# Batch 0's front of a sketched-attention kernel, rearranged: kv before the denominators, nine outer-product columns on GpSimd, one w_out product left whole

## The chip, the cores and the metric

The kernel runs on one core of a Trainium2 chip. The metric is the device time of one execution, in microseconds (us); several executions are timed and their median is given. A core has five engines with queues of their own: TensorE (PE; its weight loads are listed as PEld), VectorE (DVE), ScalarE (ACT), GpSimd (POOL) and SyncE (SP, which here only issues DMAs). Each takes its instructions in the order of the program and waits on semaphores for the other engines' results and for DMA landings.

## The reference

Polynomial-sketch attention, then a gated feed-forward layer with a sigmoid gate:

```python
# q, k, v: (4 batches, 4 heads, 1088 tokens, 32); S1, S2: (8, 32)
def phi(x):                       # 64 features a token
    a = einsum('rd,bhsd->bhsr', S1, x)
    b = einsum('rd,bhsd->bhsr', S2, x)
    return einsum('bhsi,bhsj->bhsij', a, b).reshape(..., 64)
q_p, k_p = phi(q), phi(k)
kv  = einsum('bhsf,bhsd->bhfd', k_p, v)
z   = sum(k_p, axis=2)
num = einsum('bhsf,bhfd->bhsd', q_p, kv)
den = einsum('bhsf,bhf->bhs', q_p, z)[..., None] + 1e-06
x   = (num / den) as (4352 tokens, 128)
gate = 1 / (1 + exp(-(x @ w_gate)));  val = x @ w_val    # w: (128, 1536)
out = (gate * val) @ w_out                               # w_out: (1536, 128)
```

The inputs arrive as 64-bit floats. The kernel loads them as pairs of 32-bit words; for S1, S2 and the three weight matrices it builds 32-bit floats from both words.

## The kernel before

**Staging.** The attention of a batch gives 1088 columns of `xT` (128 channels by 4352 tokens). The feed-forward layer walks over the tokens in chunks of 512 and, within a chunk, over 12 blocks of 128 hidden units. One step of it is a wave (`w1`, L556): gate and val products of a block for a chunk, then the sigmoid on ACT (`sg`, L564), the product `g` on DVE (L599), and later the block's w_out product. For the first chunk that is `w2` (L425), into the PSUM tile `moeout`; for the others it is a scheme with fewer products (L381). `slot` deals out waves one by one between pieces of the next batches' attention. A w_out product of the first chunk is emitted two waves after its own wave.

**Order.** The order within PE, DVE, ACT and POOL is that of the program text. The DMAs of SP stand in the order of their emission too. The start, batch 0, is written out by hand and is what the change rearranges.

**Loads.** The loads of the start go out on SP (k on ACT's queue): S, q's first 16 rows a partition (`T0`), gate and val of block 0, v in four parts, gate and val of block 1, w_out of blocks 0 and 1 (`load_w_out(0)`), q's other 18 rows, and then, for each pair of blocks, gate, val and w_out.

**Batch 0's front**, in the order of the text:
- `turn_q(0, 0)` turns q's first half on DVE (L673); `kps` multiplies k by the sketches (L693) and turns the results on DVE (L703) into `kab`, one half for each pair of heads.
- `ab` makes the sketches of q in PSUM (`aps`, `bps`, L800); ACT copies the first (`asb`, L810), DVE multiplies the two (`mult00`, `mult10`, L819) into `qp`.
- `gram` (L716) makes, with `spread_z` and `mask_z`, batch 0's z: ACT's copy `gs`, POOL's masking `gh` (L727), a spreading matmul (L739), then DVE's `zm` and `zb` (L750, L762).
- `outer` (L772) makes the 64 features of k for columns j0 to j1 of the nine that one pair of heads has (`kp`, 128 elements a column): by default on DVE, or on POOL.
- `kv0` (L899) adds up v times `kp` into `kvz`, for each column one matmul for each of the four heads; `kvd` copies the result (ACT, L934), `ndt` turns it on PE (`ndps`, L968) and copies it (`nd`, L985).
- `dn(0, 0, rest)` makes the denominators of the first 512 tokens (`dps`, L1083), calls `rest`, and makes the numerators (`nps`, L1102). `rest` holds the turn of the denominators (`dT`, L1094), their copy with eps (`rc`, L1224) and steps of the weights' conversion. `divide` then takes the reciprocal (L1116), spreads it (`rb`, L1131) and writes two halves of `xT` (L1121), with `head1` between.
- `head1` holds the turn of q's second half, conversion steps, and `qcomp` and `spread`: a product of q's second half with the sketches (`cqps`, L839), its copy (`cq`, L847), and four DMAs by way of DRAM (one out, three back) that make the operands of `qmult(0, 1)` (L892), which comes much later.

**Conversion of the weights.** `step(name, n)` runs one step on part n. Parts 0 and 1 are gate and val of blocks 0 and 1, part 2 is w_out of both, part 3 and every further one are the three matrices of one block (part 3 is block 2). The steps: `bounds` (ACT L140, then POOL L141), `lower` (ACT L152; for part 3 DVE L148), `shift` (DVE L157), `total` (POOL L162), `sign` (ACT L168), `final` (DVE L171, writes `w_sb`). A wave waits for its block's `final`.

Of the kernel before, what the change touches and what calls it, by code (L numbers as in the profile page):

```python
# [16 lines left out]
P = 128  # L17
# [3 lines left out]
def kernel(  # L21
# [12 lines left out]
    nc = tc.nc  # L34

    B, H, S, D = q.shape
# [4 lines left out]
    NJ = DFF // P  # L41
# [4 lines left out]
    NJK = 9  # L46
# [146 lines left out]
    def load_w_in(j0, j1):  # L193
        cs = slice(j0 * P, j1 * P)
        n, jj = divmod(j0, 2)
        if wide and jj == 0:
            w_in[n] = raw.tile([P, 3, 2, P, 2], I32, tag="w_in", name="w_in")
        for i, src in enumerate((moe_w_gate, moe_w_val)):
            if wide:
                nc.sync.dma_start(  # L200
                    out=w_in[n][:, i, jj : jj + j1 - j0].rearrange("p j m w -> p (j m w)"),
                    in_=src[:, cs].bitcast(I32),
                )
            else:
                nc.sync.dma_start(
                    out=w_sb[:, i, j0:j1].rearrange("p j m -> p (j m)"), in_=src[:, cs]
                )

    def load_w_out(n):
        j0, j1 = 2 * n, 2 * n + 2  # L210
        cs = slice(j0 * P, j1 * P)
        src = moe_w_out[cs, :].bitcast(I32) if wide else moe_w_out[cs, :]
        nc.sync.dma_start(
            out=w_in[n][:, 2].rearrange("p j m w -> p j (m w)") if wide else w_sb[:, 2, j0:j1],
            in_=src.rearrange("(j p) m -> p j m", p=P),
        )
# [26 lines left out]
    def load_rows(src, b, t, parts=((0, T, nc.sync),)):  # L243
        for t0, t1, eng in parts:
            eng.dma_start(
                out=t[:, t0:t1, :],
                in_=bass.AP(
                    tensor=src.tensor,
                    offset=src[b, 0].offset + t0 * D,
                    ap=[[T * D, P], [1, (t1 - t0) * D]],  # L250
                ),
            )
# [33 lines left out]
    load_w_in(0, 1)  # L286
    load_v(0)
    load_w_in(1, 2)
    load_w_out(0)
    load_rows(q, 0, q_t[0], ((T0, T, nc.sync),))  # L290
    for n in range(1, NJ // 2):
        load_w_in(2 * n, 2 * n + 2)
        load_w_out(n)
# [124 lines left out]
    def w2(ci, j0, jn, g):  # L418
        if j0 == 0:
            moe["sum"] = ci  # L420
            moe["acc"] = pso.tile([P, TCH], F32, tag="acc0", name="moeout")
        for jj in range(jn):
            j = j0 + jj
            for d in (slice(0, P),) if j < NJ - 2 else (slice(0, 64), slice(64, P)):
                nc.tensor.matmul(  # L425
                    out=moe["acc"][d],
                    lhsT=w_sb[:, 2, j, d],
                    rhs=g[:, jj],
                    start=(j == 0),
                    stop=(j == NJ - 1),  # L430
                )
        if j0 + jn == NJ:
            o_sb = sbA.tile([P, TCH // 32, 32], F32, tag="o_sb", name="o_sb")
            nc.vector.transpose(out=o_sb.rearrange("p t d -> p (t d)"), in_=moe["acc"])
            moe["store"] = lambda: store(
                ci, lambda g4: o_sb[32 * g4 : 32 * g4 + 32], nc.scalar
            )
# [245 lines left out]
    def kps(b):  # L683
        t = ps2.tile([P, 2, 512], F32, tag="two", name="kps")
        ts = [t[:, 0], t[:, 1]]
        turns = [(g, pi) for g in range(4) for pi in range(2)]

        if b == 0:
            ts[1] = pso.tile([P, TCH], F32, tag="acc1", name="kps1")
            turns.sort(key=lambda x: x[1])  # L690
        for g, pi in turns:
            rows = slice(64 * pi, 64 * pi + 64)
            nc.tensor.matmul(  # L693
                out=ts[pi][32 * g : 32 * g + 32, : NJK * 32],
                lhsT=sk[rows, :],
                rhs=kT_of[b][rows, KBASE[g] : KBASE[g] + NJK],
                start=True,
                stop=True,
            )

        KAB[b] = sbA.tile([P, 2, NJK, 32], F32, tag="kab", name="kab")
        for pi in range(2):
            nc.vector.transpose(  # L703
                out=KAB[b][:, pi].rearrange("p j c -> p (j c)"), in_=ts[pi][:, : NJK * 32]
            )
        KP[b] = sbA.tile([P, 2, NJK, 2, F], F32, tag="kp", name="kp", bufs=1)
# [62 lines left out]
    def outer(b, pi, j0=0, j1=NJK, eng=nc.vector):  # L769
        a0 = KAB[b][:, pi, j0:j1]  # L770
        ap = [list(a0.ap[0]), [2 * R, 2 * (j1 - j0)]]
        eng.tensor_tensor(  # L772
            out=KP[b][:, pi, j0:j1].rearrange("p j m (i l) -> p (j m) i l", i=R),
            in0=bass.AP(tensor=a0.tensor, offset=a0.offset, ap=ap + [[1, R], [0, R]]),
            in1=bass.AP(tensor=a0.tensor, offset=a0.offset + R, ap=ap + [[0, R], [1, R]]),
            op=MUL,
        )
# [6 lines left out]
    def ab(a_of=None, b_of=None, pool_b=None):  # L784

        mm = []
        if a_of is not None:
            aps = psm.tile([P, 2, 512], F32, tag="wave", name="aps")
            mm.append((a_of, aps, sa))
        if b_of is not None:  # L790
            pool, tag = (ps2, "two") if pool_b is None else pool_b
            bps = pool.tile([P, 2, 512], F32, tag=tag, name="bps")
            mm.append((b_of, bps, sb))
        for c in range(2):
            for m in range(2):
                for (bb, pr, n), dst, sx in mm:
                    h = 2 * pr + m
                    rows = slice(32 * h, 32 * h + 32)
                    t0, tn = q_chk[n]
                    nc.tensor.matmul(  # L800
                        out=dst[64 * c : 64 * c + 64, m, : 32 * tn],
                        lhsT=sx[rows, :],
                        rhs=qT_of[bb][rows, t0 : t0 + tn, c, :],
                        start=True,
                        stop=True,
                    )
        if a_of is not None:
            w = 32 * q_chk[a_of[2]][1]
            ASB[a_of] = sbA.tile([P, 2, 256], F32, tag="asb", name="asb", bufs=2)
            nc.scalar.copy(out=ASB[a_of][:, :, :w], in_=aps[:, :, :w])  # L810
        if b_of is not None:

            def mult():
                bb, pr, n = b_of
                if bb not in QP:
                    QP[bb] = sbA.tile([P, 2 * H * W1], F32, tag="qp", name="qp")
                t0, tn = q_chk[n]
                w = 32 * tn
                nc.vector.tensor_tensor(  # L819
                    out=half(QP[bb], n).rearrange("p (m c) w -> p c m w", m=2)[:, pr],  # L820
                    in0=bps[:, :, :w],
                    in1=ASB[b_of][:, :, :w],
                    op=MUL,
                )

            return mult
# [64 lines left out]
        q0 = half(QP[b], n)  # L891
        nc.vector.tensor_tensor(out=q0, in0=q0, in1=half(BQ[b], n), op=MUL)  # L892

    def kv0(j_list):
        if 0 not in KVZ:
            KVZ[0] = pso.tile([P, TCH], F32, tag="acc1", name="kvz")
        for j in j_list:
            for h in range(H):
                nc.tensor.matmul(  # L899
                    out=KVZ[0][32 * h : 32 * h + 32, :F],  # L900
                    lhsT=v_sb[:, h, j, :],
                    rhs=KP[0][:, h // 2, j, h % 2, :],
                    start=(j == 1),
                    stop=(j == NJK - 1),
                    skip_group_check=True,
                )
# [290 lines left out]
    sa, sb = sab  # L1197
    turn_q(0, 0)
    kps(0)
    ab((0, 0, 0))  # L1200
    ab((0, 1, 0))
    spread_z, mask_z = gram()
    mult00 = ab(None, (0, 0, 0))
    mult10 = ab(None, (0, 1, 0), (psm, "wave"))
    for pi in range(2):
        outer(0, pi, NJK - 3, NJK, eng=nc.gpsimd)
    step("bounds", 0, 1)
    step("lower", 0, 1)
    spread_z()
    for pi in range(2):  # L1210
        outer(0, pi, 0, 5)
    kv0([1, 2, 3, 4, 0])
    mult00()
    mult10()
    mask_z()


    def rest(turn, rc, dT):
        for pi in range(2):
            outer(0, pi, 5, NJK - 3)  # L1220
        kv0(range(5, NJK))
        turn()
        nt = rc.shape[1] - 1
        nc.scalar.activation(out=rc[:, :nt], in_=dT[:, :nt, :2], func=ACTF.Identity, bias=eps)  # L1224
        kvd(0)
        step("shift", 0, 1)
        step("total", 0, 1)
        step("sign", 0, bank="acc0")
        ndt(0)

    divide = dn(0, 0, rest)

    def head1():
        turn_q(0, 1)
        step("final", 0)
        step("sign", 1, bank="acc1")
        step("bounds", 2)
        step("lower", 2)
        step("bounds", 3)
        spread(0, (1,), qcomp(0, (1,), (psm, "wave")), nc.sync, nc.sync)  # L1240

    divide((0, 4), (4, 8), between=head1)
    step("final", 1)
# [170 lines left out]
```

## Time and profile before

| | us |
|---|---|
| three runs, median (lowest to highest) | 290.52 (290.42 to 290.61) |
| the profiled execution's own time | 289.88 |
| its span, first to last instruction | 288.1 |
| PE busy in it, 2262 matmul records | 282.3 (98%) |
| DVE / ACT / POOL busy | 171.2 / 106.7 / 159.7 |

The granted TensorE clock was 1.00 throughout. A product in 32-bit floats shows as two matmul records, so that 512 columns take two records that start 0.43 us apart. Rows of the timeline begin with the start and the duration in us; "x2" merges neighbours of one kind, and a bracket at the end gives the engine's idle time before the row and what ended it.

Marks of the front: kps at 5.96, `kab`'s two turns at 6.72, DVE's outer products at 7.49, POOL's at 9.07, `zb` at 10.45, dps at 10.81, dT at 11.51, the first `xT` at 13.96, the first wave at 14.44, the first w_out product at 17.99, block 2's wave at 18.85.

### The profile page before, as it was taken

To read this page: it belongs to the slowest core of one execution; us is meant where nothing else is said; L and a number is where in the kernel's file an instruction comes from. 1 tells how busy PE (TensorE), PEld (TensorE's weight loads), DVE (VectorE), ACT (ScalarE), POOL (GpSimd) and SP (SyncE) were. 2 spreads that over 40 slices of the span, in tenths; PEclk is the share of its full clock that TensorE was granted. 3 is DMA by queue.
4 is the path that set the end of the run, shared out by engine and by line. 5 is a ranking of instruction groups with operands and counts; after the bars stand their busy time and mean duration, and the time that the engine had idled before them with its cause. 6 is when DMAs were issued, how large, how long until landed. Compare 5 with 4: busy or idle time off the path is not lost.

```text
span 288.1 us, 5789 instructions
## 1 busy us (share of the span) xinstructions
PE 282.3 (98%) x2262; PEld 134.4 (47%) x2262; DVE 171.2 (59%) x294; ACT 106.7 (37%) x215; POOL 159.7 (55%) x222
## 2 busy tenths in 40 slices
PE   8799999999999999999999999999999999999995
PEld 3454433354444444535444445444444444444685
DVE  6987788946748547668446485767245223522571
ACT  3788832222334322523244222532243224421341
POOL 2666682667466387383565496483564646555200
PEclk9999999999999999999999999999999999999999
DMA  7995441765700386451000673020001000020012
GB/s 215 338 371 122 111 156 43 167 143 126 207 2 2 77 192 155 108 164 29 1 0 12 159 181 102 2 30 9 0 3 23 14 2 0 4 35 1 0 19 40
DMA packets 28891, 24.24 MB, mean 84 GB/s; under 512 B 18560, under 2 KB 24064, under 8 KB 28864
## 3 DMA queue, kind: packets, MB, share of 16 engines
q1 hardware_dynamic: 25888, 22.10, 29.8%
q10 hardware_dynamic: 2976, 1.77, 2.1%
q8 instruction: 18, 0.29, 0.5%
q14 instruction: 9, 0.07, 0.1%
HBM read 20.60 MB, written 3.26 MB: 83 GB/s over the span
## 4 chain that ended last, share of the span: by engine, by line
PE 97%; ACT 1%; DVE 1%; issue 0%; POOL 0%
PE wave L556 61%; PE prod L381 22%; PE moeout L425 4%; PE moeout L451 2%; PE warm L301 2%; PE kvz L912 1%; PE nps L1271 1%; PE kps L693 1%; PE cqps L839 1%; PE nps L1102 0%; PE denj L1041 0%; PE dps L1083 0%; PE nps L1054 0%; ACT asb L810 0%; DVE qp L819 0%; PE aps L800 0%
## 5 line engine op out<-in xcount | busy, mean ns | idle before, releaser
L556 PE MATMUL wave<-xT,w_sb 128*64 128x512 f32 (+3 forms) x820 | 201.4, 565 | 0.0
L564 ACT ACTIVATE sg<-wave 128x512 f32<-128x512 f32 x102 | 60.9, 597 | 158.0 <-PE wave L556 152.0
L599 DVE TENSOR_TENSOR g<-wave,sg 128x512 f32<-128x512 f32 x96 | 66.0, 688 | 87.6 <-ACT sg L564 86.1
L371 POOL TENSOR_TENSOR tsum<-g,tsum 128x256 f32<-128x256 f32 x84 | 67.5, 804 | 71.0 <-DVE g L599 70.8
L556 PEld LDWEIGHTS wave<-xT,w_sb 128*64 128x64 f32 (+1 forms) x820 | 71.0, 140 | 72.5 <-issue 53.0
L371 POOL TENSOR_TENSOR tsum<-g 128x256 f32<-128x256 f32 x84 | 67.5, 804 | 22.3 <-DVE g L599 21.7
L381 PE MATMUL prod<-tsum,ws 128*64 128x256 f32 x252 | 68.4, 380 | 0.0
L381 PE MATMUL prod<-g,w_sb 128*64 128x256 f32 (+1 forms) x170 | 50.3, 378 | 0.0
L381 PEld LDWEIGHTS prod<-tsum,ws 128*64 128x64 f32 x252 | 34.0, 137 | 13.1 <-issue 9.7
L381 PEld LDWEIGHTS prod<-g,w_sb 128*64 128x64 f32 x170 | 23.0, 137 | 30.1 <-issue 25.8
L381 PE MATMUL prod<-tsum,w_sb 128*64 128x256 f32 x84 | 25.0, 380 | 0.0
L381 PE MATMUL prod<-g,ws 128*64 128x256 f32 x84 | 25.0, 379 | 0.0
L162 POOL TENSOR_TENSOR head<-head,tail 128x384 int32<-128x384 int32 (+1 forms) x13 | 13.2, 1022 | 4.3 <-DVE head L157 4.3
L381 PEld LDWEIGHTS prod<-g,ws 128*64 128x64 f32 x84 | 11.5, 137 | 5.7
L425 PE MATMUL moeout<-g,w_sb 128*128 128x512 f32 (+1 forms) x28 | 12.4, 600 | 0.0
L381 PEld LDWEIGHTS prod<-tsum,w_sb 128*64 128x64 f32 x84 | 11.3, 137 | 1.3 <-issue 1.0
L892 DVE TENSOR_TENSOR qp<-qp,bq 128x1152 f32<-128x1152 f32 (+1 forms) x7 | 10.5, 1502 | 0.3 <-DMA bq<-dq 0.3
L772 DVE TENSOR_TENSOR kp<-kab 128x1152 f32<-128x1152 f32 (+2 forms) x10 | 10.7, 1081 | 0.0
L592 DVE TENSOR_TENSOR g<-wave,sg 128x512 f32<-128x512 f32 x6 | 6.8, 1132 | 6.3 <-ACT sg L564 4.7
L496 DVE TENSOR_TENSOR res<-prod,other 128x256 f32<-128x256 f32 x14 | 5.9, 425 | 6.3 <-ACT other L487 4.8
L141 POOL TENSOR_SCALAR head<-cap 128x384 f32<-128x384 f32 (+1 forms) x13 | 6.3, 487 | 5.2 <-ACT cap L140 5.2
L152 ACT ACTIVATE tail<-w_in,two__157 128x384 f32<-128x384 uint32 (+1 forms) x12 | 7.2, 610 | 0.0
(130 smaller groups left out, 196.0 us busy)
## 6 DMA issues: line engine op xcount, KB each, us to landing
qp<-dq SPq DMA_DIRECT2D x7, 576.0 KB
bq<-dq SPq DMA_DIRECT2D x14, 288.0 KB
kq<-in_k_dram SPq DMA_DIRECT2D x3, 544.0 KB
kq<-in_q_dram SPq DMA_DIRECT2D x3, 544.0 KB
w_in<-in_moe_w_out_dram SPq DMA_DIRECT2D x6, 256.0 KB
w_in<-in_moe_w_gate_dram SPq DMA_DIRECT2D x5, 256.0 KB
w_in<-in_moe_w_val_dram SPq DMA_DIRECT2D x5, 256.0 KB
v<-in_v_dram SPq DMA_DIRECT2D x8, 144.0 KB
```

The costliest lines, as they stand in the source:

```text
L141: nc.gpsimd.tensor_scalar(out=self.head.bitcast(F32), in0=self.cap, scalar1=122880.0, scalar2=2.0**-15, op0=ALU.min, op1=ALU.max,)
L152: nc.scalar.activation(out=self.tail, in_=self.lo, func=ACTF.Identity, bias=two, scale=2.0**-51)
L162: nc.gpsimd.tensor_tensor(out=self.head, in0=self.head, in1=self.tail.bitcast(I32), op=ALU.add)
L371: nc.gpsimd.tensor_tensor(out=t[:, u], in0=in0, in1=in1, op=ALU.subtract)
L381: nc.tensor.matmul(out=out, lhsT=lhsT, rhs=rhs, start=start, stop=stop, skip_group_check=True)
L425: nc.tensor.matmul(out=moe["acc"][d], lhsT=w_sb[:, 2, j, d], rhs=g[:, jj], start=(j == 0), stop=(j == NJ - 1),)
L556: nc.tensor.matmul(out=wv[d, which, jj * tw + o : jj * tw + o + tp], lhsT=w_sb[:, which, j0 + jj, d], rhs=xT[:, t0 + o : t0 + o + tp], sta ...
L564: nc.scalar.activation(out=sg, in_=wv[:, 0], func=ACTF.Sigmoid)
L592: nc.vector.tensor_tensor(out=g.rearrange("p (j u s y) -> p j y u s", j=2, u=2, y=4), in0=wv[:, 1].rearrange("p (j y u s) -> p j y u s", j ...
L599: nc.vector.tensor_tensor(out=g, in0=wv[:, 1], in1=sg, op=MUL)
L772: eng.tensor_tensor(out=KP[b][:, pi, j0:j1].rearrange("p j m (i l) -> p (j m) i l", i=R), in0=bass.AP(tensor=a0.tensor, offset=a0.offset, ...
L892: nc.vector.tensor_tensor(out=q0, in0=q0, in1=half(BQ[b], n), op=MUL)
```

## The change

In words: q's second half is loaded before w_out of blocks 0 and 1. POOL makes columns 4 to 8 for the first pair of heads, ahead of `gh`, and columns 5 to 8 for the second pair after it; DVE makes the other nine in two instructions where it made twelve in four. All of `kv0` is emitted ahead of `dn`: columns 1, 2, 3 and 0 for all heads, then columns 4 to 8 for heads 0 and 1, then for heads 2 and 3. The turn of q's second half and `kvd` follow `mask_z`; `ndt` comes first in `rest`. In `head1`, `qcomp` and `spread` stand before `lower` of part 2 and `bounds` of part 3. In `w2`, only block 11's product is still made in two halves of 64 rows; block 10's is whole.

```diff
@@ loads
     load_w_in(1, 2)
+    load_rows(q, 0, q_t[0], ((T0, T, nc.sync),))
     load_w_out(0)
-    load_rows(q, 0, q_t[0], ((T0, T, nc.sync),))
@@ w2
-            for d in (slice(0, P),) if j < NJ - 2 else (slice(0, 64), slice(64, P)):
+            for d in (slice(0, P),) if j < NJ - 1 else (slice(0, 64), slice(64, P)):
@@ kv0
-    def kv0(j_list):
+    def kv0(j_list, heads=range(H)):
...
-            for h in range(H):
+            for h in heads:
@@ batch 0's front
     turn_q(0, 0)
     kps(0)
+
+    by_pool = (NJK - 5, NJK - 4)
+    outer(0, 0, by_pool[0], NJK, eng=nc.gpsimd)
     ab((0, 0, 0))
     ab((0, 1, 0))
     spread_z, mask_z = gram()
     mult00 = ab(None, (0, 0, 0))
     mult10 = ab(None, (0, 1, 0), (psm, "wave"))
-    for pi in range(2):
-        outer(0, pi, NJK - 3, NJK, eng=nc.gpsimd)
+    outer(0, 1, by_pool[1], NJK, eng=nc.gpsimd)
     step("bounds", 0, 1)
     step("lower", 0, 1)
     spread_z()
     for pi in range(2):
-        outer(0, pi, 0, 5)
-    kv0([1, 2, 3, 4, 0])
+        outer(0, pi, 0, by_pool[pi])
+    kv0([1, 2, 3, 0])
+    kv0(range(4, NJK), (0, 1))
+    kv0(range(4, NJK), (2, 3))
     mult00()
     mult10()
     mask_z()
+    turn_q(0, 1)
+    kvd(0)
 
     def rest(turn, rc, dT):
-        for pi in range(2):
-            outer(0, pi, 5, NJK - 3)
-        kv0(range(5, NJK))
+        ndt(0)
         turn()
...
-        kvd(0)
         step("shift", 0, 1)
         step("total", 0, 1)
         step("sign", 0, bank="acc0")
-        ndt(0)
...
     def head1():
-        turn_q(0, 1)
         step("final", 0)
         step("sign", 1, bank="acc1")
         step("bounds", 2)
+        spread(0, (1,), qcomp(0, (1,), (psm, "wave")), nc.sync, nc.sync)
         step("lower", 2)
         step("bounds", 3)
-        spread(0, (1,), qcomp(0, (1,), (psm, "wave")), nc.sync, nc.sync)
```

## The prediction

> **What bounds the kernel now.** First the chain that ended last: TensorE (PE) holds it for 97%, and its feed-forward lines L556, L381 and L425 alone make 87%. Then busy time by stretch, cut where the first feed-forward matmul starts (14.44 us), where block 2's wave starts (18.85) and where block 10's w_out product comes up (45.21). The columns are stretch, length, then busy us and count by engine, granted TensorE clock, DMA share and GB/s.
>
> ```profile
> 0.00:14.44 14.44, 11.94 (x201) 5.98 (x201) 11.71 (x37) 7.36 (x20) 6.31 (x21) 1.00 0.92 277
> 14.44:18.85 4.41, 4.41 (x19) 2.65 (x16) 3.88 (x10) 3.88 (x8) 2.75 (x5) 1.00 1.07 374
> 18.85:45.21 26.36, 26.36 (x83) 11.08 (x81) 20.79 (x38) 17.47 (x35) 19.38 (x29) 1.00 0.49 144
> ```
>
> From 14.44 to 45.21 PE's busy time equals the stretch, and after that the chain is PE too. So the change moves the end in two ways only: by when the first waves can start (then by any pause put between them), and by PE work saved later. Both pass through to the end one for one. Third, the timeline of the first 20 us, engine by engine.
>
> **Block 10's product.** The second view is PE's timeline around 45 us.
>
> ```profile
> 42.63 1.02 PE L425 MATMUL moeout<-g,w_sb 128*128 128x512 f32 x2
> 43.49 1.88 PE L556 MATMUL wave<-xT,w_sb 128*128 128x512 f32 x4
> 45.30 1.08 PE L425 MATMUL moeout<-g,w_sb 128*64 128x512 f32 x4
> 46.31 0.72 PE L693 MATMUL kps<-kT,sk 64*32 64x288 f32 x16
> ```
>
> A whole product takes 43.49 - 42.63 = 0.86. The wave in front of block 10 ends at 43.49 + 2 x 0.86 = 45.21, so the halved product costs 0.09 until it starts and 1.01 until kps starts, 1.10 in all. The whole one costs 0.86 and then the pause before kps, whose tiles differ from it: about 0.10, as the 0.09 here. So 0.14 is saved. Bounds: 0.05 (only 1.01 against 0.96) to 0.24 (no pause at all).
>
> **Nine columns on GpSimd (POOL).** Before, POOL makes two times three columns from 9.07 to 10.72, beside VectorE's (DVE's) two qp products, and DVE makes ten columns from 7.49 and two more at 10.58. Afterwards POOL makes five of head pair 0 as soon as `kab`'s first half is turned (6.72 + 0.48 = 7.20; from such a DVE end POOL started 0.15 later at 12.28, so about 7.3), that is, ahead of DVE's own columns at 7.49. Price by the only POOL row of this operation, 384 elements in 0.84: some 0.14 of lead (below) and 1.8 ns each, so 1.31 to 1.40 (in proportion) for 640 elements, of which I take 1.35, and 1.10 for 512.
>
> The question is whether that lies beside DVE's columns. These rows say no:
>
> ```profile
> 8.19 0.82 DVE L772 TENSOR_TENSOR kp<-kab 128x640 f32<-128x640 f32 x1
> 8.65 0.46 POOL L727 TENSOR_TENSOR gh<-gs,e_m 128x32 f32<-128x32 f32 x1 [2.37 <-ACT gs L725]
> 10.69 0.43 POOL L141 TENSOR_SCALAR head<-cap 128x256 f32<-128x256 f32 x1
> 10.79 0.48 DVE L772 TENSOR_TENSOR kp<-kab 128x128 f32<-128x128 f32 x1
> 103.37 1.35 DVE L772 TENSOR_TENSOR kp<-kab 128x1152 f32<-128x1152 f32 x1
> 103.53 1.78 POOL L371 TENSOR_TENSOR tsum<-g 128x256 f32<-128x256 f32 x1
> ```
>
> POOL's gh has 32 elements and lasts until 9.11, 0.10 after DVE's columns end at 9.01. A tsum that mostly takes 0.73 takes 1.78 and ends at 105.31, 0.59 after DVE's columns (104.72), so 0.14 of it was its lead. The other way round, DVE's 128-element column at 10.79 ends at 11.27, 0.15 after POOL's instruction ends at 11.12, against 0.28 for its twin. Whichever comes second waits for the whole instruction of the first, then needs about 1.06 ns an element on DVE (0.15 for 128). At 55 to 57 us they take turns.
>
> So afterwards: POOL 7.31 to 8.66; DVE's four columns (512 x 1.06 = 0.54) to 9.21 instead of 8.09; gh to 9.31; DVE's five (0.68) to 9.99; POOL's four (1.10 - 0.14) to 10.96. The two qp products follow at 9.97 and 10.58 (before 8.99 and 9.60), zm at 11.18, zb 11.43 to 11.65 (before 10.45 to 10.67): 0.98 late. Behind the columns in POOL's queue stand bounds 0 and 1 (0.83 for both), done at 11.8; the totals that need them come at 13.4.
>
> The Trainium skill ("SBUF — State Buffer", "Who interferes with whom") has it that a DVE instruction with two inputs in SBUF and a GpSimd one that reads SBUF exclude each other for the length of an instruction, whoever issued first. By the 0.84 row taken alone, measured beside products that read PSUM, the nine columns would be free; the rule speaks against that, and against this part of the change.
>
> **kv ahead of the denominators.** The kvz rows step 0.111 a column with four heads at once (9.50 to 10.05 for five). With two heads at once a column still takes 0.11, as each head's matmuls queue behind their own: 4 + 5 + 5 columns are 1.55 where nine were 1.0. From DVE's last column: 10.06 + 0.44 + 0.56 = 11.06, then the second pairs (POOL done 10.96) to 11.6. dps needs zb, 11.65 + 0.14 as before = 11.79, so the longer kv costs nothing while zb is that late; with zb at the old time it would set dps at 11.0 instead of 10.81.
>
> **q's turn and the rest up to the first wave.** The turn of q's second half (0.66) leaves the gap between rb and final 0 and lies at 11.56 to 12.24, where DVE waits for dps anyway (its dT starts at dps + 0.70 = 12.49). Its data: by SP's waits (explained below) q's second half landed at about 11.05, just ahead of the issue at 11.07; one 256 KB load earlier is about 10.3, 0.7 being the step of such landings. It may be 1.2 later before the turn waits, and then costs one for one after the 0.25 that dT leaves free. w_out(0) takes the place at 11.05 and is first used at 13.9. kvd, the turned copy (ndps 0.33, nd 0.27) and nps come to 13.1 to 13.8, no longer the limit. From dT on, with the old rows: shift +0.37 and +0.54, reciprocal +0.82, rb +1.11, final 0 at +1.57 (it now waits for POOL's total, 0.73, begun 0.15 after the first shift), first xT +1.88, first wave +2.36 where it was 14.44 - 11.51 = 2.93. So 12.49 + 2.36 = 14.85: 0.40 late, of 0.98 late at dT.
>
> **Behind the first wave.** A limit stands here already: block 2's conversion waits for its third weight load, the w_out rows of blocks 2 and 3 (issued at 8.41). SP's issue at 14.58 waited for that landing: in the view of SP's waits each issue waits for the load eight issues back.
>
> ```profile
> 14.58 0.33 SPq L200 DMA_DIRECT2D w_in<-in_moe_w_val_dram  x1
> 14.63 0.55 ACT L140 ACTIVATE cap<-w_in 128x384 f32<-128x384 f32 x1 [0.26 <-issue]
> 17.15 0.68 DVE L599 TENSOR_TENSOR g<-wave,sg 128x512 f32<-128x512 f32 x1
> 17.99 1.02 PE L425 MATMUL moeout<-g,w_sb 128*128 128x512 f32 x2
> ```
>
> The bytes ahead of that load stay the same, so 14.58 stays. Moved forward on ScalarE (ACT) are the cq copy (0.64), the 8 qcomp matmuls it follows (now 13.6 to 14.25), and on SP the four DMAs of spread; those stand behind all weight loads (18.12) either way, and qp's product at 35.91 does not wait for them. But cq (14.28) and lower 2 now stand before bounds 3: 15.3 to 15.85 instead of 14.63 to 15.19. POOL's part follows at 15.93 to 16.44, shift 3 at 16.5, lower 3 to 17.3, total 2 to 17.2, final 2 at 17.27 (before 16.81), g(0) 17.61 to 18.3. moeout(0) starts 0.16 after g, 18.46, a pause of 0.18 behind the two waves (14.85 + 3.44); final 3 ends at 19.05, hidden behind moeout. Block 2's wave starts at 19.32 instead of 18.85: 0.47 late. Later finals have 0.65 and more of slack.
>
> **Sum.** Span 288.10 + 0.47 - 0.14 = 288.43; the profiled execution took 289.88, of which 1.78 lie around the span, so 290.21. The runs' median is 290.52, 0.64 above that execution; shifted alike, **290.85**, or +0.1%. A measurement of this kernel can tell about 0.2% (0.58) from no change, so this is no change with a lean to slower.
>
> **Rivals.**
> *The columns do lie beside each other (faster).* For it: POOL's 0.84 rows were not stretched. Against: the six rows shown. Then DVE's columns end at 8.87, dps is set by the longer kv (11.0), dT 11.70, first wave 14.05. But the load at 14.58 holds bounds 3 and so shift 3 (15.84), final 2 (16.58) and g(0) (ends 17.60): moeout(0) at 17.76, 0.23 early, not 0.39. With 0.14: **290.15**.
> *GpSimd's columns are dearer than the 384 row (slower).* The place is POOL's first instruction: DVE's columns wait for all of it, so each 0.1 on it is 0.1 on zb and on all that follows. For it: POOL's subtractions take 0.73 for 256 elements, 2.8 ns each; 640 elements 1.8, 512 1.45. Against: same operation, same shape at 1.8 to 2.2. Then 9.11, DVE 9.65, gh 9.75, DVE 10.43, POOL 11.74; the second pairs of kv end at 12.36 and set dps, dT 13.06, first wave 15.42, 0.98 late, block 2's wave by 0.07 more as in the forecast: **291.43**. It is slower by over 0.2% from about 1.6 us for that instruction.
> *The start is a wash and only block 10 counts.* If POOL waits behind DVE's first columns, or gh slips behind the second, but the late final 2 is made good by shorter waits, the first wave stays near 14.44: **290.4**.
>
> **Chances.** Forecast 0.45, free columns 0.20, dearer columns 0.23, wash 0.12. Faster by over 0.2% needs more than the 0.53 that even the free case gives without the load's limit: 0.10. Slower takes the dearer case and the upper tail of the forecast: 0.33. Within: 0.57. The range runs from the free case to the dearer one, **290.1 to 291.5**.
>
> **What would show it.** Right: POOL's 640-element row from 7.3 to about 8.7, DVE's first columns 1.1 longer than 0.6, zb near 11.6, first wave near 14.85, moeout at 45 us as x2 of 128*128 and 0.14 shorter with its pause. Wrong: DVE's columns at 0.6 and 0.8 beside POOL's; a first wave before 14.44; the load landing far from 14.58; PE pausing after 19.3.

## The result, and the profile after

The changed kernel took 291.01 us (median of 16 runs) against 290.04 for the kernel before, timed beside it 16 times. The ratio is 1.0032, with a 95% interval of 1.0019 to 1.0045: slower by 0.6 to 1.3 us. One of its 16 runs, in a slower state of the chip, took 295.99 and is left out of the ratio. The profiled execution of the changed kernel took 291.14 with a span of 289.1; the one before had 289.88 and 288.1.

The view by stretches, cut at the changed kernel's own marks (first feed-forward wave, block 2's wave, kps of batch 1):

```profile
5.00:14.98 9.98, 8.31 (x195) 4.62 (x194) 9.45 (x22) 5.51 (x16) 6.03 (x9) 1.00 1.07 320
14.98:19.97 4.99, 4.67 (x15) 2.65 (x16) 4.35 (x11) 4.09 (x10) 2.89 (x5) 1.00 1.06 374
19.97:47.28 27.31, 27.31 (x86) 11.47 (x84) 21.50 (x40) 17.84 (x35) 19.53 (x29) 1.00 0.45 126
```

Before, PE was busy for all of the stretch from the first wave to block 2's, 4.41 long. Now that stretch is 4.99 long and PE is idle in it for 0.3 by this view's account. The rest is full, as before. So the span's extra 0.97 us must lie ahead of 19.97.

Start times in the timelines split it. kab is the first turn of the sketches of k (L703): what lies ahead of it is loads, S's conversion and kps, of which the change touches only the order of two loads.

| stretch, us | before | after | forecast |
|---|---|---|---|
| start to kab | 6.72 | 7.03 | no change |
| kab to zb | 3.73 | 4.54 | +0.98 |
| zb to dT | 1.06 | 1.07 | 0 |
| dT to first wave | 2.93 | 2.34 | -0.57 |
| first wave to block 2's wave | 4.41 | 4.99 | +0.07 |
| block 2's wave to kps of batch 1 | 27.46 | 27.31 | -0.14 |
| kps of batch 1 to the end | 241.79 | 241.79 | 0 |

The last row is the same to a hundredth: nothing behind 47 us has changed. Without the first row the change costs 0.66. The first row's 0.31 is mostly there before the two exchanged loads are issued (at 5.97 before and 6.44 after): DVE's first turn of k (`kT`, L662) already starts at 4.48 instead of 4.27.

**The front.** The changed kernel's timeline of DVE and POOL:

```profile
7.59 1.29 POOL L772 TENSOR_TENSOR kp<-kab 128x640 f32<-128x640 f32 x1 [1.10 <-DVE kab L703]
7.80 1.63 DVE L772 TENSOR_TENSOR kp<-kab 128x512 f32<-128x512 f32 x1
8.94 0.59 POOL L727 TENSOR_TENSOR gh<-gs,e_m 128x32 f32<-128x32 f32 x1
9.36 0.85 DVE L772 TENSOR_TENSOR kp<-kab 128x640 f32<-128x640 f32 x1
9.49 1.65 POOL L772 TENSOR_TENSOR kp<-kab 128x512 f32<-128x512 f32 x1
```

Each row ends after the one above it. POOL's five columns end at 8.88. DVE's four were issued at 7.80 and end at 9.43, 0.55 after POOL is done: they waited 1.1 us for work of 0.55. gh ends 0.10 after DVE's columns, DVE's five end 0.68 after gh, and POOL's four 0.93 after those.

**Behind the first wave.** The shifts of parts 2 and 3 and POOL's instructions beside them, in the kernel before:

```profile
15.27 0.51 POOL L141 TENSOR_SCALAR head<-cap 128x384 f32<-128x384 f32 x1 [0.82 <-ACT cap L140]
15.44 0.48 DVE L157 TENSOR_SCALAR head<-head 128x256 int32<-128x256 int32 x1
15.84 0.34 DVE L157 TENSOR_SCALAR head<-head 128x384 int32<-128x384 int32 x1
16.00 0.77 POOL L162 TENSOR_TENSOR head<-head,tail 128x256 int32<-128x256 int32 x1 [0.23 <-DVE head L157]
```

DVE, POOL and PE in the changed kernel, from part 2's shift to the first w_out product:

```profile
15.99 0.28 DVE L157 TENSOR_SCALAR head<-head 128x256 int32<-128x256 int32 x1
16.14 0.51 POOL L141 TENSOR_SCALAR head<-cap 128x384 f32<-128x384 f32 x1 [0.95 <-ACT cap L140]
16.62 0.73 POOL L162 TENSOR_TENSOR head<-head,tail 128x256 int32<-128x256 int32 x1
16.69 0.87 DVE L157 TENSOR_SCALAR head<-head 128x384 int32<-128x384 int32 x1 [0.41 <-POOL head L141]
17.48 0.54 DVE L148 TENSOR_SCALAR tail<-w_in 128x384 f32<-128x384 uint32 x1
17.94 0.41 DVE L171 TENSOR_TENSOR w_sb<-square,head 128x256 f32<-128x256 f32 x1
18.27 0.68 DVE L599 TENSOR_TENSOR g<-wave,sg 128x512 f32<-128x512 f32 x1
19.00 1.12 PE L425 MATMUL moeout<-g,w_sb 128*128 128x512 f32 x2 [0.31 <-DVE g L599]
```

The row to see is shift of part 3 at 16.69: 0.87 instead of 0.34 before. It ends at 17.56, 0.21 after POOL's total of part 2 at 17.35. Both were set free by POOL's instruction at 16.14, and POOL, which needed no signal from itself, was 0.07 ahead. Before, total of part 2 still waited for shift of part 2, so that shift of part 3 went first. The sign of it was already in the trace before: shift of part 2, which takes 0.28 in the changed kernel, took 0.48 there and ended 0.14 after POOL's instruction at 15.27. PE's last row shows g as what it waited for. Of the 0.58 by which the stretch grew, 0.47 lies in front of that product (4.02 behind the first wave instead of 3.55), and 0.11 between it and block 2's wave (0.97 instead of 0.86).

In the profile, the chain of work that ended last now gives 6% to DMAs, all ahead of 17.49, where it steps from lower of part 3 (L148) to a landing. That row has no idle time in front of it: DVE was busy with the long shift until 17.56. The step is not a wait.

**Block 10's product**, PE's timeline:

```profile
44.61 1.88 PE L556 MATMUL wave<-xT,w_sb 128*128 128x512 f32 x4
46.33 1.02 PE L425 MATMUL moeout<-g,w_sb 128*128 128x512 f32 x2
47.28 0.72 PE L693 MATMUL kps<-kT,sk 64*32 64x288 f32 x16
```

The product follows its wave without a pause (44.61 + 4 x 0.43 = 46.33), and kps comes 0.95 later, where the halved one took 1.10 with its pause.

### The profile page after: what moved, and what is told of

Read it like the earlier page. It is cut to its first block, busy times and chain, and to the rows that moved or that the text cites. A ratio compares the mean times of both kernels' runs of the same rounds, so it can differ in the third digit from the quotient of the medians.

```text
span 289.1 us, 5783 instructions
## 1 busy us (share of the span) xinstructions
PE 283.1 (98%) x2260; PEld 135.1 (47%) x2260; DVE 171.6 (59%) x292; ACT 106.8 (37%) x215; POOL 161.1 (56%) x222
## 4 chain that ended last, share of the span: by engine, by line
PE 92%; DMA 6%; DVE 1%; issue 0%
PE wave L556 60%; PE prod L381 22%; PE moeout L425 4%; PE moeout L451 2%; DMA v<-in_v_dram 2%; DMA w_in<-in_moe_w_val_dram 2%; DMA w_in<-in_moe_w_gate_dram 2%; PE kvz L912 1%; DMA kq<-in_k_dram 1%; PE nps L1272 1%; PE kps L693 1%; PE cqps L839 1%; PE denj L1041 0%; PE nps L1054 0%; DVE g L599 0%; PE ndps L977 0%
## 5 line engine op out<-in xcount | busy, mean ns | idle before, releaser
L371 POOL TENSOR_TENSOR tsum<-g,tsum 128x256 f32<-128x256 f32 x84 | 68.6, 817 | 71.0 <-DVE g L599 70.8
L371 POOL TENSOR_TENSOR tsum<-g 128x256 f32<-128x256 f32 x84 | 66.6, 792 | 22.1 <-DVE g L599 21.5
L425 PEld LDWEIGHTS moeout<-g,w_sb 128*128 128x128 f32 (+1 forms) x26 | 4.3, 181 | 6.5 <-issue 3.7
```

The costliest lines, as they stand in the source:

```text
L371: nc.gpsimd.tensor_tensor(out=t[:, u], in0=in0, in1=in1, op=ALU.subtract)
L425: nc.tensor.matmul(out=moe["acc"][d], lhsT=w_sb[:, 2, j, d], rhs=g[:, jj], start=(j == 0), stop=(j == NJ - 1),)
```

## The experiments

Each kernel ran beside the kernel before on the same chip; ratios are against that. The last columns are the marks of each one's profiled execution.

| kernel | ratio, 95% interval | kab at | kab to zb | kab to first wave | first to block 2's wave | to kps |
|---|---|---|---|---|---|---|
| before | | 6.72 | 3.73 | 7.72 | 4.41 | 27.46 |
| changed | 1.0032, 1.0019 to 1.0045 | 7.03 | 4.54 | 7.95 | 4.99 | 27.31 |
| after_again | 1.0031, 1.0021 to 1.0040 | 6.88 | 4.54 | 7.95 | 4.98 | 27.31 |
| b10_alone | 1.0004, 0.9995 to 1.0012 | 7.10 | 3.73 | 7.72 | 4.41 | 27.31 |
| nine_alone | 1.0071, 1.0044 to 1.0098 | 6.63 | 4.55 | 10.26 | 5.11 | 27.46 |
| six_columns | 1.0024, 1.0010 to 1.0038 | 6.80 | 3.92 | 7.68 | 5.00 | 27.31 |
| spread_back | 1.0008, 1.0000 to 1.0017 | 6.97 | 4.55 | 7.96 | 4.40 | 27.31 |
| lower_first | 1.0038, 1.0023 to 1.0052 | 7.15 | 4.54 | 7.95 | 4.76 | 27.31 |
| one_by_one | 1.0075, 1.0058 to 1.0092 | 6.82 | 4.41 | 10.01 | 4.99 | 27.31 |
| six_spread | 1.0002, 0.9981 to 1.0022 | 7.06 | 3.92 | 7.68 | 4.41 | 27.30 |
| six_spread_load | 1.0003, 0.9994 to 1.0012 | 6.83 | 3.91 | 7.68 | 4.40 | 27.31 |
| six_den_first | 1.0010, 1.0001 to 1.0018 | 6.84 | 3.92 | 7.92 | 4.40 | 27.31 |
| six_split | 0.9992, 0.9983 to 1.0000 | 6.62 | 3.92 | 7.56 | 4.41 | 27.31 |
| six_split_again | 0.9988, 0.9978 to 0.9997 | 6.77 | 3.92 | 7.56 | 4.41 | 27.31 |

The marks repeat to a few hundredths wherever the code is the same; what scatters is kab, from 6.62 to 7.15.

### The changed kernel again: after_again

> The changed kernel once more, beside the three that follow. Theory: from kab's first turn to the first wave 7.95 us (7.72 before), from the first wave to block 2's wave 4.98 (4.41 before), shift of part 3 at 0.87 behind total of part 2, block 10's mark 0.15 earlier; together 0.65 us slower than before, the rest of the 0.97 of the first profile being the start in front of kab, which differs from execution to execution. Rival (the start in front of kab is later in every execution of the changed kernel): kab at 7.0 or later again.

All marks came back, shift of part 3 at 0.88, and kab at 6.88 instead of 7.03. 0.65 from the code is shown twice.

### Block 10 alone: b10_alone

```diff
-            for d in (slice(0, P),) if j < NJ - 2 else (slice(0, 64), slice(64, P)):
+            for d in (slice(0, P),) if j < NJ - 1 else (slice(0, 64), slice(64, P)):
```

> The kernel before with one edit: block 10's w_out product made whole. Theory: 0.14 us saved where it stands (its two matmul records at 128*128, no pause in front of them, the pause before kps stays), passed on to the end: 0.05 to 0.24 us faster than before, the front unchanged. Rival (the halves were there for a reason, a pause opens elsewhere around 45 us): 0 or slower.

The mark shows the 0.15, but the time does not: a ratio of 1.0004, whose interval just reaches that saving at 0.9995. In its profiled execution kab came at 7.10, 0.38 late, more than the saving. The saving is shown in the trace only.

### The nine columns alone: nine_alone

```diff
     kps(0)
+    by_pool = (NJK - 5, NJK - 4)
+    outer(0, 0, by_pool[0], NJK, eng=nc.gpsimd)
...
-    for pi in range(2):
-        outer(0, pi, NJK - 3, NJK, eng=nc.gpsimd)
+    outer(0, 1, by_pool[1], NJK, eng=nc.gpsimd)
...
-        outer(0, pi, 0, 5)
-    kv0([1, 2, 3, 4, 0])
+        outer(0, pi, 0, by_pool[pi])
+    kv0([1, 2, 3, 0])
...
-        for pi in range(2):
-            outer(0, pi, 5, NJK - 3)
-        kv0(range(5, NJK))
+        kv0(range(4, NJK))
```

> The kernel before with only the nine columns on GpSimd (five ahead of gh, four after it; kv, q's turn, loads and the order in head1 as before). Theory (the two engines exclude each other for whole instructions): VectorE's first columns end about 1.1 us later, zb 0.98 later, and with q's turn still in the chain the first wave too: 0.9 to 1.0 us slower than before. Rival (the columns do lie beside each other): VectorE's columns take 0.6 and 0.8, 0.0 to 0.2 us faster.

zb came 0.82 late, as in the changed kernel: the columns do not lie beside each other. The time came out larger than expected, by something new. The view by stretches of 2 us (the granted clock is third from the right):

```profile
10.00:12.00 2.00, 0.96 (x36) 0.63 (x36) 1.36 (x4) 0.76 (x2) 1.47 (x3) 0.88 1.03 377
12.00:14.00 2.00, 1.69 (x48) 1.25 (x40) 1.28 (x5) 0.56 (x3) 0.54 (x1) 0.50 1.07 375
14.00:16.00 2.00, 1.58 (x21) 0.80 (x25) 1.21 (x3) 1.72 (x7) 1.14 (x3) 0.50 1.06 375
16.00:18.00 2.00, 2.00 (x11) 0.93 (x4) 1.86 (x6) 1.43 (x4) 0.67 (x3) 0.50 1.06 373
```

PE's clock falls to a half from 12 to 18 us. In three of six executions the mean clock was 0.988 and the time 293.0 to 293.2; in one it was 0.994 and the time 292.12; in two it was 1.000 and the time 290.75 and 290.93, which is 0.7 to 0.9 above before and near the 0.9 to 1.0 expected.

### Columns as before: six_columns

```diff
-    by_pool = (NJK - 5, NJK - 4)
-    outer(0, 0, by_pool[0], NJK, eng=nc.gpsimd)
...
-    outer(0, 1, by_pool[1], NJK, eng=nc.gpsimd)
+    for pi in range(2):
+        outer(0, pi, NJK - 3, NJK, eng=nc.gpsimd)
...
-        outer(0, pi, 0, by_pool[pi])
-    kv0([1, 2, 3, 0])
-    kv0(range(4, NJK), (0, 1))
-    kv0(range(4, NJK), (2, 3))
+        outer(0, pi, 0, NJK - 3)
+    kv0([1, 2, 3, 4, 5, 0])
+    kv0(range(6, NJK), (0, 1))
+    kv0(range(6, NJK), (2, 3))
```

> The changed kernel with GpSimd's columns back to three and three, after gh; VectorE makes twelve in two instructions; all else of the change stays. Theory: zb about 0.8 us earlier than in the changed kernel, first wave about 0.6 earlier (near the 14.4 of before); but the cq copy and lower of part 2 still stand ahead of bounds of part 3, so that shift of part 3 still meets GpSimd's total of part 2: 0.2 to 0.4 us slower than before, 0.5 to 0.7 faster than the changed kernel. Rival (kv ahead of the denominators is what costs): zb earlier, but dps not, and the time stays within 0.2 of the changed kernel's.

Against the changed kernel zb is 0.62 earlier, the first wave only 0.27, where 0.6 was expected: the longer kv now holds dps (0.57 behind zb, not 0.36), so a part of the rival is true. The stretch behind the first wave stays at 5.00, so the two losses are apart: the columns cost the first wave, something else the second.

### spread back behind the conversion: spread_back

```diff
-        spread(0, (1,), qcomp(0, (1,), (psm, "wave")), nc.sync, nc.sync)
         step("lower", 2)
         step("bounds", 3)
+        spread(0, (1,), qcomp(0, (1,), (psm, "wave")), nc.sync, nc.sync)
```

> The changed kernel with qcomp and spread back behind bounds of part 3. Theory: the first wave stays where the changed kernel has it; bounds of part 3 ends 0.6 us earlier on ScalarE, shift of part 3 runs ahead of total of part 2 again (0.36 us instead of 0.87), and the pause of 0.48 us before the first w_out product falls to 0.1: 0.4 to 0.5 us faster than the changed kernel, 0.3 to 0.6 slower than before. Rival (the pause comes from the late g alone, by way of the first wave): no change against the changed kernel.

The first wave stayed (7.96), and all of the 0.58 behind it went. DVE and POOL in this kernel:

```profile
15.29 0.51 POOL L141 TENSOR_SCALAR head<-cap 128x384 f32<-128x384 f32 x1 [0.15 <-ACT cap L140]
15.93 0.55 DVE L157 TENSOR_SCALAR head<-head 128x256 int32<-128x256 int32 x2
16.30 1.73 POOL L162 TENSOR_TENSOR head<-head,tail 128x256 int32<-128x256 int32 x2 [0.50 <-DVE head L157]
```

bounds of part 3 is over at 15.80, before the shifts begin; both shifts take 0.55 together, and the totals wait for them. This move of one line past two others is the larger part of the loss.

### lower ahead of the shifts: lower_first

```diff
-    step("shift", 2, 3)
     step("lower", 3, eng=nc.vector)
+    step("shift", 2, 3)
```

> The changed kernel with lower of part 3 ahead of the two shifts on VectorE. Theory (shift of part 3 loses 0.5 us behind GpSimd's total of part 2, because that total is ready first): now shift of part 2 ends later than bounds of part 3, total of part 2 follows it and shift of part 3 goes first at about 0.36 us; the first w_out product starts 0.2 to 0.4 us earlier after the first wave, 0.2 to 0.4 faster than the changed kernel. Rival (the pause comes from bounds of part 3 alone): shift 3 short, but the pause stays at 0.48 and so does the time.

Here shift of part 3 goes ahead of POOL's total of part 2 without bounds having moved:

```profile
16.57 0.64 DVE L157 TENSOR_SCALAR head<-head 128x256 int32<-128x256 int32 x2
17.02 1.73 POOL L162 TENSOR_TENSOR head<-head,tail 128x256 int32<-128x256 int32 x2 [0.23 <-DVE head L157]
```

Both shifts take 0.64 and the stretch falls from 4.98 to 4.76. The 0.22 is not all that the meeting costs: with shift of part 2 now behind lower of part 3, total of part 2 starts 1.92 behind the first wave instead of 1.64, and DVE stands idle for 0.61 before final of part 2, waiting for that total. So this order trades one delay for another. How the 0.58 divides between the meeting and the late bounds, no run shows; together they are the whole of it, as spread_back removes both. In the times nothing of the 0.22 is to be seen (1.0038 against 1.0031, intervals overlapping; kab was late in the profiled execution). The expected gain is shown in the trace, not in the time.

### GpSimd's columns one by one: one_by_one

```diff
-    outer(0, 0, by_pool[0], NJK, eng=nc.gpsimd)
+    for j in range(by_pool[0], NJK):
+        outer(0, 0, j, j + 1, eng=nc.gpsimd)
```

> The changed kernel with GpSimd's first five columns in five instructions of one column each. Theory (the second comer waits for one whole instruction of the first, and they take turns): VectorE's first columns end at 1.4 to 1.6 us after kab's first turn instead of 2.4, its second at about 2.4 instead of 3.2; but GpSimd's columns and gh end later (gh near 3.5 instead of 2.5), so dps comes 0.2 to 0.5 later than in the changed kernel: not faster than it. Rival (VectorE is slowed by anything that GpSimd does beside it, by the element and not by the instruction): VectorE's first columns end at 2.4 as before the split.

DVE and POOL, kab at 6.82:

```profile
7.38 0.41 POOL L772 TENSOR_TENSOR kp<-kab 128x128 f32<-128x128 f32 x1 [1.00 <-DVE kab L703]
7.59 0.75 DVE L772 TENSOR_TENSOR kp<-kab 128x512 f32<-128x512 f32 x1
7.75 0.85 POOL L772 TENSOR_TENSOR kp<-kab 128x128 f32<-128x128 f32 x1
8.26 1.02 DVE L772 TENSOR_TENSOR kp<-kab 128x640 f32<-128x640 f32 x1
```

DVE's first columns end 1.51 after kab instead of 2.40, its second 2.46 instead of 3.18. The wait is as long as one instruction of the other engine and they take turns: POOL's second column takes 0.85, as it waits for DVE's 512 elements. gh moved to 3.65 after kab, so nothing was gained. dps came 1.30 later than in the changed kernel, and not 0.2 to 0.5. PE waited 1.5 us for gh, and its clock fell to a half again (0.50 from 12 to 14 us). The ratio is 1.0075; in the two executions at full clock it was 291.46 and 291.73.

### Putting the parts together: six_spread, six_spread_load, six_den_first, six_split

six_spread joins six_columns and spread_back.

> Six columns on GpSimd as before and qcomp and spread back behind bounds of part 3; loads, kv ahead, q's turn and block 10 as changed. Theory: kab to first wave 7.68, first wave to block 2's wave 4.41, block 10 0.15: the parts add up, 0.1 to 0.3 us faster than before. Rival (the parts do not add up; the kernel's start or another wait takes it back): no faster than before.

By its marks it should be 0.2 faster than before; the time shows no difference, and with an interval of 0.4% it can't. The parts do add up in the trace.

six_spread_load also puts the loads back:

```diff
-    load_rows(q, 0, q_t[0], ((T0, T, nc.sync),))
     load_w_out(0)
+    load_rows(q, 0, q_t[0], ((T0, T, nc.sync),))
```

> As six_spread, with q's second half loaded behind w_out of blocks 0 and 1 again. Theory (the order of these two loads costs and brings nothing: q's second half lands at 11.05, its turn comes at 10.9 to 11.7): kab to first wave 7.7, the time within 0.2 us of six_spread's. Rival (the changed order of loads delays the start in front of kab): kab back at 6.7, 0.2 to 0.3 us faster than six_spread.

Same marks, same time: the order of the two loads is worth nothing here. kab at 6.83 and not 6.7 speaks against the rival, though one profile doesn't settle it.

six_den_first puts the last columns of kv, kvd and ndt back behind dps:

```diff
-    kv0(range(6, NJK), (0, 1))
-    kv0(range(6, NJK), (2, 3))
...
-    kvd(0)
...
-        ndt(0)
+        kv0(range(6, NJK))
         turn()
...
+        kvd(0)
         step("shift", 0, 1)
...
+        ndt(0)
```

> As six_spread, with the last three columns of kv, kvd and ndt behind dps again as before. Theory: dps follows zb by 0.36 instead of 0.57, q's turn stays out of the chain; kab to first wave about 7.4, the load of block 2's weights (landed 13.7 to 14.6) sets the first w_out product: 0.2 to 0.4 us faster than before. Rival (kv, kvd and nps then end last): kab to first wave 7.6 or more, no gain over six_spread.

A miss, and the rival was right: dps came 0.37 behind zb, but PE then waited for kvd and nd,

```profile
12.82 0.33 PE L968 MATMUL ndps<-ident,kvd 128*128 128x128 f32 x1 [0.72 <-ACT kvd L934]
13.51 0.67 PE L1102 MATMUL nps<-qp,nd 64*32 64x256 f32 x16 [0.35 <-ACT nd L985]
```

and the first wave was 0.24 later than in six_spread. Having the last columns of kv, kvd and ndt early is thus worth something: it takes nps off the path.

six_split leaves only six matmuls of kv behind dps and puts ndt behind rc:

```diff
-    kv0(range(6, NJK), (2, 3))
...
-    kvd(0)
...
-        ndt(0)
+        kv0(range(6, NJK), (2, 3))
+        kvd(0)
         turn()
...
         step("total", 0, 1)
+        ndt(0)
         step("sign", 0, bank="acc0")
```

> As six_spread, with the last three columns of kv for the second pair of heads behind dps, and ndt behind the copy rc. Theory: dps follows zb by 0.36 instead of 0.56 and nothing else ends later: kab to first wave 7.5, 0.15 to 0.4 us faster than before. Rival (nps or the load of block 2's weights ends last then): kab to first wave 7.7, or a pause behind the first wave; no faster than six_spread.

> six_split once more, to narrow its interval. Theory: by its marks (kab to first wave 7.55 instead of 7.72, block 10's 0.15) it is 0.32 us faster than before, less what the start in front of kab adds: a ratio of 0.9985 to 0.9995. Rival (the first result was the start's scatter): a ratio whose interval is centred on 1.000.

```profile
10.91 0.64 PE L1083 MATMUL dps<-qp,zb 128*32 128x256 f32 x8
11.38 0.51 PE L899 MATMUL kvz<-kp,v 128*32 128x64 f32 x12
12.93 0.67 PE L1102 MATMUL nps<-qp,nd 64*32 64x256 f32 x16 [0.36 <-ACT nd L985]
14.18 3.71 PE L556 MATMUL wave<-xT,w_sb 128*128 128x256 f32 x12
```

dps goes 0.37 behind zb, nps is over (13.6) before the first wave, and the first wave comes 7.56 after kab. Median 289.77 against 290.01, ratio 0.9988 (0.9978 to 0.9997) in the second run: it beats both kernels, by a tenth of a percent over the one before. But something else did end later: from dT to the first wave it takes 2.57 instead of six_spread's 2.35, so that of the 0.34 gained at dT only 0.12 is left at the first wave.

## Why the prediction was right or wrong

The time, 291.01, lies in the range, and 0.16 above the point. But the point was counted up from a median of 290.52, and the kernel before, timed 16 times, has 290.04. The change was forecast at +0.33 and measured at +0.93 (0.6 to 1.3): the direction of the lean was right, "no change" was not. That the time came so near the point is luck: the base was 0.48 too high and the change, by the medians (+0.97), 0.64 too small. Term by term:

- **The nine columns**: right in mechanism, sized 0.17 too high. POOL went first, DVE's first columns waited for all of it, gh, DVE's second and POOL's second followed in the order and almost at the distances forecast. zb was 0.81 late, not 0.98: POOL's five columns took 1.29, not 1.35, and began 0.03 sooner, and the rest is spacing ahead of DVE's products. The case of columns that lie beside each other fell (six_columns, nine_alone, one_by_one), and so did that of dearer ones (1.29, not 1.8). The rule of the Trainium skill ("SBUF — State Buffer", "Who interferes with whom") that the prediction draws on held in every row of the columns, and the 0.84 row alone would have misled.
- **dT to the first wave**: 2.36 forecast, 2.34 measured. The turn of q's second half was hidden where the forecast put it, and final 0 came right behind POOL's total.
- **Behind the first wave**: this step failed. The forecast had bounds of part 3 late by cq and lower of part 2, and a pause of 0.18 in front of moeout, 0.07 in all; it then let total of part 2 and shift of part 3 run at their old lengths. The stretch grew by 0.58. In the runs shift of part 3, too, waits for POOL, as the columns do, and POOL's total of part 2 got ahead of it: 0.87 instead of 0.34, then lower, final 2 and g behind it in DVE's queue. The forecast had the shift start 1.65 behind the first wave, and it started at 1.71; but it had g at 2.76, and g started at 3.29. The 0.53 that the shift took longer is thus nearly all that the forecast missed. spread_back removes the whole 0.58, lower_first 0.22 by another order.
- **The load that "stays" at 14.58** did not: in the changed kernel's profile it landed at 13.7. That made no difference, because ACT came to bounds of part 3 only at 15.52.
- **Block 10**: 0.14 forecast, 0.15 in every trace. The time of b10_alone does not show it.
- **What stays open**: the marks give 0.65 and the runs 0.93. Some of the surplus lies outside the span, from the first instruction to the last: the kernel before has a median span of 288.2 in every later set of runs, with at most 2.0 us around it; in the first set the changed kernel's is 288.7, with 1.8 to 2.1 around it in ten executions and 2.7 to 2.9 in five. In after_again it is otherwise, 289.05 with 1.8 to 2.1 around it. In the two profiles of the changed kernel kab came 0.31 and 0.16 later than in the only profile of the kernel before, but the 14 profiles have it anywhere from 6.62 to 7.15, with either order of loads. Whether the changed kernel starts later on average, or is more often unlucky, these runs do not tell.

## What to carry to other kernels

Work given to a second engine is free only if the two do not exclude each other: look for a row of the same pair of operand kinds side by side, not for the operation's price alone, and then apply what you find to every later pair of instructions in the same chain, not only to the one you moved. A copy moved up two places in the queue of an engine that is idle for most of the kernel (ACT is busy for 106.8 of 289.1 us) can be the costlier half of a change, if the next instruction in that queue feeds another engine's chain. Cut two traces at the same events before you compare them: the total of these kernels scattered by more than most of the effects, while the distances between events repeated to hundredths.

## What the runs showed of the hardware that was not expected

- **PE's clock falls after short waits.** In nine_alone PE stood still for 1.03 us ahead of dps, in a stretch that was half idle (0.96 busy from 10 to 12 us), and the granted clock was 0.50 from 12 to 18 us; in one_by_one it was 0.50 from 12 to 14 after a stop of 1.54 ahead of z's spreading matmul. It did so in some executions and not in others, and cost 2.1 to 2.5 us in nine_alone (293.0 to 293.2 against 290.75 and 290.93). The Trainium skill ("TensorE: Matmul & The Clock Gate", "Part 1: The HAM clock gate (the "warmup" mystery)") has the clock halved after an idle window of about 3.4 us that runs freely. That the outcome changes from run to run agrees with a free-running window; that stops of 1.03 and 1.54 us were enough does not fit an idle window of 3.4 in which PE does nothing. How the chip counts a stretch that is half idle, no run here shows.
- **An integer shift with one input waits for GpSimd too**: 0.87 instead of 0.34 us, ended 0.21 after POOL's instruction. A transpose beside one of POOL's totals (12.97 to 13.70 before) was not stretched: 0.74, which is also the mean of the four of its kind.
